# Leaving out the imaginary weight of mode 0 in a banded attention and spectral mixing kernel

## The chip, the cores and the metric

The kernel runs on one core of a Trainium2 chip. The metric is the device time of one execution in microseconds (us); of several executions the median is given. The engines are named as in the profile: PE (TensorE, matrix products; PEld its weight loads), DVE (VectorE), ACT (ScalarE), POOL (GpSimd) and SP (SyncE, which here only issues DMAs). POOL also issues DMAs, on a queue of its own, and these can change the type on the way from float32 to bfloat16.

## The reference

Attention over 8 batches, 8 heads, 576 tokens and 64 values per head, each token seeing itself and the 127 before it, gives x. Then comes mixing in the frequency domain of the token axis, and a last layer:

```python
X = np.fft.rfft(x, axis=1)
Xr, Xi = (np.real(X[:, :n_modes]), np.imag(X[:, :n_modes]))
Yr = np.einsum('bmd,mde->bme', Xr, w_r) - np.einsum('bmd,mde->bme', Xi, w_i)
Yi = np.einsum('bmd,mde->bme', Xr, w_i) + np.einsum('bmd,mde->bme', Xi, w_r)
Y[:, :n_modes] = Yr + 1j * Yi
y = np.fft.irfft(Y, n=S, axis=1)
u = x + y
return (u + np.maximum(u @ w_ch, 0.0)).astype(np.float32)
```

There are 64 modes, and each has a real and an imaginary weight, w_r and w_i, of 512 x 512 float32 values, that is 1 MB (1024 KB) each and 128 MB together. For mode 0 the sum over tokens has no imaginary part, so Xi is zero there, and the inverse real transform does not read the imaginary part of Y at mode 0. In mode 0 w_i therefore stands only in one product with zero and in one value that is not read.

## The kernel before

**Two stages.** The first computes attention for 16 units (a batch and half of the heads each) in a software pipeline and leaves x and its spectrum XC in the on-chip memory. The second, the weight stage, multiplies XC with the 128 weights in order, transforms back and writes the output in a closing stage (from L695 on).

**The order of the work.** Every engine runs its instructions in the order in which the program text issues them; the schedule is written by hand. The buffers of a pool are used in turn, and a load into a used buffer waits until the matmuls on its old content are done.

**Weights and their numbers.** Weight i is w_r of mode i/2 where i is even and w_i of mode (i-1)/2 where i is odd. The list todo_w (L438) holds the numbers that are not loaded yet. load_w(n, pool, bf16, chosen) (L440) takes the next n of the list that are not in the list again, or those in chosen. With bf16 it issues the load on POOL's queue into a bfloat16 tile (L449), 512 KB; without, on SP's queue into a float32 tile of 1024 KB (L453), of which the matmuls read the upper halves as bfloat16. wq keeps the tile of each number, homes the pool.

**What is loaded where.**
- During attention, at stages that AHEAD names (L413), 14 weights go by POOL's queue into the pool early, each (but the first) behind a small copy (gate, L520) that waits for a result of the pipeline. In the stages that LATER names, 6 more go into the tiles that held q, k and v. That is 20.
- After attention SP loads into the six buffers of the pool w (NWA = 6, L533). The first number that is left is called first, and again (L532) is the list of eight numbers first + 4, first + 6, ... that POOL will load into early a second time.
- In the weight loop, after the four matmuls of weight k: as long as k < AGAIN = 8, POOL reloads an early buffer (L656); for a weight in a buffer of SP's, SP loads the next into it (L658).
- K1 (L640) is the number behind the last of again. After weight K1 - 1 the memory of early is given up; two more buffers w2 for SP and the tile wch (by POOL) are put there.

**The weight loop** (L641). Four modes share one accumulator acc of 128 rows; mode m works on 32 of them, in the group of 32 columns of PE that belongs to them (tile_position). For each weight PE does four matmuls, with a part of XC as the loaded operand:

```python
m, ri = 4 * g + i // 2, i % 2
w = wq[2 * m + ri]
for a in range(4):
    nc.tensor.matmul(acc[32 * (i // 2) : 32 * (i // 2) + 32], lhsT=XC[...], rhs=w[a],
                     start=(ri == 0 and a == 0), stop=(ri == 1 and a == 3),
                     tile_position=(0, 32 * (i // 2)))
```

After eight weights quad_end scales acc to yq (DVE at L543, ACT at L541 for the last), PE transposes it (L547), and DVE copies it to YT. From weight 64 on a list of other work, side, is taken piece by piece between the weights: four early_spectra (L575) and 36 project (L613), which multiply tokens by w_ch. After each of weights 123 to 126, where the list is empty, PE gets six matmuls whose result is not used (warm, L633).

Of the kernel before, what the change touches and what calls it, by code (L numbers as in the profile page):

```python
# [397 lines left out]
def kernel(  # L398
# [13 lines left out]
    NM, DM, _ = moe_w_r.shape  # L412
    AHEAD = {0: 1, 1: 1, 2: 1, 4: 1, 5: 1, 7: 1, 8: 1, 10: 1, 11: 1, 12: 1, 13: 3, 14: 1}  # L413
    LATER = {14: 3, 15: 3}
    EARLY, NWA, NWB, AGAIN = 14, 6, 2, 8
# [12 lines left out]
    early = actx1.enter_context(  # L428
        tc.tile_pool(name="w1", bufs=EARLY, side="right", reuse_waits="tile")
    )  # L430
# [4 lines left out]
    vflat = raw["v"].rearrange("p u s h d -> p (u s h d)")  # L435
    spare += [vflat[:, 2 * DM * i :] for i in range(3)]
    spare = [t[:, : 2 * DM].bitcast(BF16).rearrange("p (a e) -> p a e", a=4) for t in spare]
    wq, homes, todo_w, again = {}, {}, list(range(2 * NM)), []  # L438

    def load_w(n, pool, bf16, chosen=None):  # L440


        for i in ([i for i in todo_w if i not in again][:n] if chosen is None else chosen):
            todo_w.remove(i)
            src = (moe_w_r, moe_w_i)[i % 2][i // 2].rearrange("(p a) e -> p a e", a=4)
            homes[i] = pool
            if bf16:
                t = spare.pop(0) if pool is None else pool.tile([P, 4, DM], BF16, tag="w", name="w")
                nc.gpsimd.dma_start(out=t, in_=src)  # L449
                wq[i] = [t[:, a] for a in range(4)]  # L450
            else:
                t = pool.tile([P, 4, DM], FP32, tag="w", name="w")
                nc.sync.dma_start(out=t, in_=src)  # L453
                wq[i] = [t[:, a].bitcast(BF16)[:, 1::2] for a in range(4)]

    with ExitStack() as actx:
# [43 lines left out]
        for h in (0, 2):  # L500
# [4 lines left out]
        side = {0: [(at.offset, 4), (at.offset, 6), (at.decay, 5), (at.offset, 5), (at.decay, 7),  # L505
                    (at.offset, 7), (at.decay, 4), (at.decay, 6)]}
# [18 lines left out]
    with ExitStack() as mctx:  # L525
# [6 lines left out]
        again = [first + 4 + 2 * i for i in range(AGAIN)]  # L532
# [4 lines left out]
        def quad_end(acc, g):  # L537

            yq = pool.tile([P, DM], BF16, tag="yq")
            if g == NM // 4 - 1:  # L540
                nc.scalar.mul(yq, acc, 2.0 / S)  # L541
            else:
                nc.vector.tensor_scalar_mul(yq, acc, 2.0 / S if g else norm)  # L543
            yield
            tr = ps.tile([P, 4, P], BF16, tag="tr", bufs=1, name="tr")
            for et in range(4):
                nc.tensor.transpose(tr[:, et], yq[:, et * P : (et + 1) * P], ident)  # L547
            hf, mm = g // 8, 4 * (g % 8)
            for ri in range(2):
                src = tr.rearrange("p e (j c) -> p e c j", c=32)[:, :, ri * B : ri * B + B]  # L550
                dst = YT[:, hf, :, :, ri, mm : mm + 4]
                if hf == 1:
                    nc.vector.tensor_copy(dst, src)
                else:
                    for par in range(2):
                        nc.vector.tensor_copy(dst[:, :, 1 - par :: 2], src[:, :, par::2])
# [76 lines left out]
        def warm():  # L633
            wt = ps.tile([P, DM], FP32, tag="warm", bufs=1, name="warm")
            for _ in range(6):
                nc.tensor.matmul(wt, lhsT=ident, rhs=wch[:, 0], start=True, stop=True)  # L636

        quads, side = [], []
        ZW = Z = XW = wch = w2 = None
        K1 = again[-1] + 1  # L640
        for g in range(NM // 4):  # L641
            acc = ps.tile([P, DM], FP32, tag="acc", bufs=2, name="acc")
            for i in range(8):
                m, ri = 4 * g + i // 2, i % 2
                w = wq[2 * m + ri]
                for a in range(4):
                    c0 = (a * NC + (8 if ri == 0 else 0)) * NM + m
                    nc.tensor.matmul(  # L648
                        acc[32 * (i // 2) : 32 * (i // 2) + 32],
                        lhsT=XC[:, c0 : c0 + 31 * NM + 1 : NM],  # L650
                        rhs=w[a],
                        start=(ri == 0 and a == 0), stop=(ri == 1 and a == 3),
                        tile_position=(0, 32 * (i // 2)),
                    )
                k = 8 * g + i
                if k < AGAIN:  # L656
                    load_w(1, early, True, again[k : k + 1])
                elif homes[k] not in (early, None):  # L658
                    load_w(1, homes[k], False)
                if k == K1 - 1:  # L660
                    actx1.close()
                    w2 = mctx.enter_context(
                        tc.tile_pool(name="w2", bufs=NWB, side="right", reuse_waits="tile")
                    )
                    load_w(NWB, w2, False)
                    right = mctx.enter_context(
                        tc.tile_pool(name="late", bufs=1, side="right", reuse_waits="tile")
                    )
                    wch = right.tile([P, 4, DM], BF16, name="wch")
                    nc.gpsimd.dma_start(out=wch, in_=moe_w_ch.rearrange("(a p) e -> p a e", p=P))  # L670
                    ZW = right.tile([P, B // 2, 2, DM], BF16, name="ZW")
                    Z = right.tile([P, B, DM], BF16, name="Z")
                    XW = right.tile([P, len(units), 2, DM], BF16, name="XW")

                if quads:
                    if next(quads[0], True):
                        quads.pop(0)
                elif side and k % 5:
                    side.pop(0)()
                elif 8 * g + i >= 2 * NM - 5:  # L680
                    if 8 * g + i < 2 * NM - 1:
                        warm()
            end = quad_end(acc, g)
            next(end)
            quads.append(end)
            if g == 7:
                side += [partial(early_spectra, bp) for bp in range(B // 2)]
                side += [partial(project, j, n) for j in range(len(units)) for n in range(2)]
# [132 lines left out]
```

The softmax here doesn't subtract the row's maximum and nothing guards it: scores larger than these inputs give would overflow.

## Time and profile before

| | |
|---|---|
| median of nine runs | 457.98 us (456.46 to 459.09) |
| the profiled execution's own time | 459.09 us |
| its span in the profile | 457.3 us |
| its mean granted PE clock | 0.906 of full speed |
| PE busy | 358.9 us (78%) |
| DVE, ACT, POOL busy | 173.6, 154.8, 54.3 us |
| matmuls of the weights, acc (L648) | 488 recorded as reading the tiles w, 145.7 us |
| DMA packets | 158.31 MB, mean 346 GB/s |
| SP's queue (hardware_dynamic) | 142.62 MB, 81.2% of 16 engines over the span |
| POOL's queue (software_dynamic) | 15.21 MB, 16.8% |
| issues of weights by SP | 54 of w_i and 46 of w_r, 1024 KB each, 18.7 and 18.3 us to landing (median) |
| issues of weights by POOL into early | 15 of w_r and 7 of w_i, 512 KB each; six more into the tiles of q, k and v |

Attention takes the first 134 us or so; the first matmul of a weight starts at 134.46 us and the last ones at 414.07 us.

How to read it: the span is the profiled stretch on the core; the execution's own time is a little longer. The lines of the profile give start and duration in us, the engine, the line of the kernel (L648 is line 648), the operation and the tiles that it writes and reads, then how often. A bracket behind a line holds the idle time of the engine before it and what ended that. The chain of waits is the sequence of work that ended last, followed back from the end.

### The profile page before, as it was taken

What the parts mean: (1) busy time and instruction counts of PE and PEld (TensorE: products, weight loads), DVE (VectorE), ACT (ScalarE), POOL (GpSimd) and SP (SyncE); (2) the same over time, 40 slices, a digit from 0 to 9 for tenths busy, and PEclk for the clock granted to TensorE, in tenths of its full rate; (3) what the DMA queues carried; (4) which work ended last, traced back from release to release, by engine and by line L of the source; (5) the groups of instructions that cost most, each with busy time, mean ns of one, the idle gap of its engine ahead of it and who ended that gap; (6) DMA issues with size and microseconds to landing.
All of it is one profiled execution on the core that took longest, in us unless ns stands there. A gap on an engine that the chain in (4) does not pass through costs nothing.

```text
span 457.3 us, 7803 instructions
## 1 busy us (share of the span) xinstructions
PE 358.9 (78%) x3269; PEld 189.5 (41%) x3292; DVE 173.6 (38%) x314; ACT 154.8 (34%) x191; POOL 54.3 (12%) x86
## 2 busy tenths in 40 slices
PE   5678999998867656566666799998989898987793
PEld 4456777776654212122221244443433343433230
DVE  7988699998832101000010142111111111202684
ACT  6869799998810000000000021121111121204572
POOL 8510001012402100000000000000000000000562
PEclk9989899999999778866677589999999899999998
DMA  8999999999999999999999999999999999990598
GB/s 281 323 335 302 293 257 314 314 301 240 203 286 315 313 318 316 335 387 425 420 421 419 423 421 418 420 421 421 421 419 420 421 421 418 421 412 24 191 346 290
DMA packets 51874, 158.31 MB, mean 346 GB/s; under 512 B 3712, under 2 KB 22656, under 8 KB 39040
## 3 DMA queue, kind: packets, MB, share of 16 engines
q1 hardware_dynamic: 47280, 142.62, 81.2%
q0 software_dynamic: 4560, 15.21, 16.8%
q8 instruction: 25, 0.41, 0.4%
q14 instruction: 9, 0.07, 0.0%
HBM read 163.58 MB, written 9.44 MB: 378 GB/s over the span
## 4 chain that ended last, share of the span: by engine, by line
DMA 56%; PE 24%; DVE 10%; ACT 4%; issue 3%; POOL 1%; ACTq 0%; DVEq 0%; POOLq 0%; SPq 0%
DMA w<-in_moe_w_i_dram 33%; DMA w<-in_moe_w_r_dram 13%; PE acc L648 7%; DMA vr<-in_moe_w_i_dram 6%; DMA qr<-in_q_dram 5%; PE av L332 3%; PE my L623 2%; PE tp L251 2%; DVE x L348 1%; DVE vb L234 1%; DVE q L239 1%; DVE o L766 1%; PE warm L636 1%; PE yy L752 1%; DVE att L306 1%
## 5 line engine op out<-in xcount | busy, mean ns | idle before, releaser
L648 PE MATMUL acc<-w,XC 128*32 128x512 bf16 x488 | 145.7, 449 | 53.6 <-DMA w<-in_moe_w_r_dram 34.6
L648 PEld LDWEIGHTS <-XC 128*32 128x32 bf16 x512 | 59.6, 140 | 128.0 <-issue 95.7
L295 ACT ACTIVATE att<-sc 128x1024 bf16<-128x1024 f32 x64 | 64.1, 1033 | 9.6 <-PE sc L285 9.6
L629 ACT CAST XW<-my 128x512 bf16<-128x512 f32 x36 | 21.1, 587 | 108.0 <-PE my L587 108.0
L733 POOL TENSOR_TENSOR r<-r,x 128x1024 f32<-128x1024 f32 x8 | 17.0, 2131 | 274.2 <-ACT r L731 274.1
L571 ACT CAST ZW<-zw 128x512 bf16<-128x512 f32 x4 | 2.3, 587 | 137.0 <-PE zw L566 137.0
L543 DVE TENSOR_SCALAR yq<-acc 128x512 bf16<-128x512 f32 x14 | 9.7, 690 | 98.6 <-PE acc L648 98.6
L611 DVE COPY xT<-tr 128x1024 bf16<-128x1024 bf16 x18 | 12.5, 692 | 89.5 <-PE tr L609 89.5
L332 PE MATMUL av<-vb,att 128*128 128x132 bf16 (+1 forms) x576 | 38.4, 217 | 8.1 <-DVE x L348 5.4
L332 PEld LDWEIGHTS <-att 128*128 128x128 bf16 x704 | 36.6, 98 | 13.5 <-DVE x L348 9.9
L623 PE MATMUL my<-wch,xT 128*64 128x512 bf16 x288 | 38.7, 391 | 0.8 <-DVE xT L611 0.8
L257 ACT COPY qkT<-tp 128x1152 bf16<-128x1152 bf16 x30 | 33.5, 1118 | 3.2 <-PE tp L251 2.5
L285 PE MATMUL sc<-qkT 64*64 64x256 bf16 (+2 forms) x640 | 25.3, 265 | 5.1 <-ACT qkT L257 1.2
L348 DVE TENSOR_TENSOR x<-av,rec 128x640 bf16<-128x640 f32 x32 | 26.4, 825 | 1.1
L766 DVE TENSOR_TENSOR o<-yy,r 128x1024 f32<-128x1024 f32 (+1 forms) x20 | 21.8, 1115 | 8.0 <-PE yy L752 3.9
L623 PEld LDWEIGHTS <-xT 128*64 128x64 bf16 x288 | 13.4, 110 | 23.3 <-issue 9.9
L285 PEld LDWEIGHTS <-qkT 64*64 64x64 bf16 x640 | 14.6, 109 | 19.3 <-issue 16.3
L234 DVE CAST vb<-vr 64x1024 bf16<-64x1024 f32 x32 | 22.2, 694 | 0.2
L306 DVE TENSOR_TENSOR att<-att,mask 128x1024 bf16<-128x1024 bf16 x32 | 20.6, 685 | 0.0
L731 ACT ACTIVATE r<-mm 128x1024 f32<-128x1024 f32 (+1 forms) x19 | 17.8, 979 | 6.6 <-PE mm L587 6.5
L272 PE MATMUL sc<-bias,ident 128*128 128x512 bf16 x48 | 16.7, 402 | 1.4 <-ACT att L295 1.4
L520 POOL COPY gate<-x 1x1 bf16<-1x1 bf16 x11 | 5.4, 490 | 88.6 <-DVE x L348 88.6
(105 smaller groups left out, 333.1 us busy)
## 6 DMA issues: line engine op xcount, KB each, us to landing
w<-in_moe_w_i_dram SPq DMA_DIRECT2D x54, 1024.0 KB, 18.7
w<-in_moe_w_r_dram SPq DMA_DIRECT2D x46, 1024.0 KB, 18.3
qr<-in_q_dram SPq DMA_DIRECT2D x16, 576.0 KB, 8.6
kr<-in_k_dram SPq DMA_DIRECT2D x16, 576.0 KB, 8.5
vr<-in_v_dram SPq DMA_DIRECT2D x32, 256.0 KB, 7.6
w<-in_moe_w_r_dram POOLq DMA_DIRECT2D x15, 512.0 KB, 21.2
out_dram<-o SPq DMA_DIRECT2D x15, 512.0 KB, 3.8
w<-in_moe_w_i_dram POOLq DMA_DIRECT2D x7, 512.0 KB, 8.3
```

Source lines behind the costliest of these rows:

```text
L234: nc.vector.tensor_copy(self.vb[u % 2][row, :, :, :, W * half : W * half + D], src[row, :2])
L257: (self.nc.vector.tensor_copy if u < 2 and w == "q" else self.nc.scalar.copy)(dst.rearrange("q h (p j) -> q h p j", j=TPP), tp.rearrange(" ...
L285: nc.tensor.matmul(sc[64 * half : 64 * half + 64, e, j * 256 + c0 : j * 256 + c0 + n], lhsT=qkT[row, 1, h, k0 + j : k0 + P : 2], rhs=qkT[r ...
L295: self.nc.scalar.activation(self.att[u % 2][:, kt * 8 * P : (kt + 1) * 8 * P], sc.rearrange("p e n -> p (e n)"), AF.Exp, scale=1.0 / math. ...
L306: nc.vector.tensor_tensor(out=rows, in0=rows, in1=self.table[:, heads], op=ALU.mult)
L332: nc.tensor.matmul(bank[:, qt * W : qt * W + rhs[j].shape[1]], lhsT=att[:, o : o + P], rhs=rhs[j], start=(n == 0 and j == 0), stop=(n == l ...
L348: nc.vector.tensor_tensor(out=self.x[:, b, :, cs].rearrange("p t (h d) -> p h t d", h=2), in0=tiles[:, :, :, :D], in1=rec.unsqueeze(-1).br ...
L623: nc.tensor.matmul(mm[ROWS[half]], lhsT=lhsT, rhs=wch[:, dt], start=(dt == 0), stop=False, skip_group_check=True,)
L629: nc.scalar.copy(XW[:, j, n], mm)
L648: nc.tensor.matmul(acc[32 * (i // 2) : 32 * (i // 2) + 32], lhsT=XC[:, c0 : c0 + 31 * NM + 1 : NM], rhs=w[a], start=(ri == 0 and a == 0), ...
L731: nc.scalar.activation(r[:, part], mm[:, part], AF.Relu)
L766: nc.vector.tensor_tensor(out=o[:, c], in0=yy[:, c], in1=r[:, c], op=ALU.add)
```

## The change

Number 1, which is w_i of mode 0, is taken out of todo_w. In the loop a number that was never loaded is passed over before its matmuls, with all that stands behind it in the loop's body. Since weight 0 is then the only one of mode 0, its fourth matmul ends the accumulation. The reloads no longer go by the number k < 8 but by a copy of again, recycle, of which each weight that is multiplied takes one until it is empty.

```diff
-    wq, homes, todo_w, again = {}, {}, list(range(2 * NM)), []
+    wq, homes, todo_w, again = {}, {}, [0, *range(2, 2 * NM)], []
@@
-        quads, side = [], []
+        quads, side, recycle = [], [], list(again)
@@
                 m, ri = 4 * g + i // 2, i % 2
+                if 2 * m + ri not in wq:
+                    continue
                 w = wq[2 * m + ri]
@@
-                        start=(ri == 0 and a == 0), stop=(ri == 1 and a == 3),
+                        start=(ri == 0 and a == 0), stop=(ri == (m > 0) and a == 3),
@@
                 k = 8 * g + i
-                if k < AGAIN:
-                    load_w(1, early, True, again[k : k + 1])
+                if recycle:
+                    load_w(1, early, True, [recycle.pop(0)])
                 elif homes[k] not in (early, None):
```

The lists that follow from todo_w, worked out from the text of both kernels:

| | before | after |
|---|---|---|
| loaded during attention (20) | 0 to 19 | 0, 2 to 20 |
| first | 20 | 21 |
| again (8, by POOL) | 24, 26, ... 38 | 25, 27, ... 39 |
| K1 | 39 | 40 |
| loaded by SP | 100 | 99 |

## The prediction

> **What bounds the kernel now.** I read the page from its slices down. The rows for TensorE (PE), the granted clock, the DMA engines and their rate, 40 slices of 11.43 us each:
>
> ```profile
> PE   5678999998867656566666799998989898987793
> PEclk9989899999999778866677589999999899999998
> DMA  8999999999999999999999999999999999990598
> GB/s 281 323 335 302 293 257 314 314 301 240 203 286 315 313 318 316 335 387 425 420 421 419 423 421 418 420 421 421 421 419 420 421 421 418 421 412 24 191 346 290
> ```
>
> The DMA row is full until slice 36. From slice 18 (206 us) the rate is flat at 418 to 425 GB/s, and it does not move when PE goes from six tenths busy to nine, nor when the clock goes from 0.5 to 0.9. A rate that ignores PE is set by the transfers. Before slice 17 it is lower, 313 to 318 GB/s, with the DMA row just as full: both queues run there. The windows of the weight stage say the same (span, busy time and count of PE, PEld, DVE, ACT and POOL, granted clock, DMA share, rate):
>
> ```profile
> 153.00:192.00 39.00, 23.49 (x83) 9.03 (x80) 2.62 (x10) 0.00 (x0) 0.82 (x2) 0.78 1.04 318
> 192.00:214.00 22.00, 13.51 (x41) 4.84 (x40) 1.31 (x5) 0.00 (x0) 0.00 (x0) 0.70 1.04 400
> 235.00:256.00 21.00, 14.50 (x40) 4.57 (x38) 1.31 (x5) 0.00 (x0) 0.00 (x0) 0.66 1.01 422
> 300.00:350.00 50.00, 44.35 (x287) 19.81 (x288) 7.20 (x13) 8.22 (x14) 0.00 (x0) 1.00 1.01 421
> ```
>
> Then the chain of waits, to see what PE does when a weight arrives. In 192 to 256 us it alternates a DMA of 18 us with four matmuls; its end is this:
>
> ```profile
> 385.33 18.75 DMA w<-in_moe_w_i_dram
> ...
> 404.13 1.07 PE acc L648 x4
> ...
> 405.35 1.24 PE warm L636 x5
> ...
> 406.61 1.07 PE acc L648 x4
> 407.68 1.40 PE warm L636 x6
> ...
> 409.10 1.07 PE acc L648 x4
> ...
> 414.07 1.08 PE acc L648 x4
> ```
>
> The last wait for a transfer ends at 404.13, with weight 123. From there PE runs weight, warm burst, weight without a gap, one per (414.07 - 404.13) / 4 = 2.485 us, which is also the pace of the transfers. Behind 415 us lies a closing stage of 42 us that reads no weight. So the end is: arrival of weight 123, plus a fixed tail.
>
> **The change, part by part.** I number weights 2m for w_r and 2m + 1 for w_i of mode m. Weight 1 drops out of the list todo_w. Since load_w takes the next of the list and not a named one, no issue place goes empty in the attention stage: the POOL issue at 25.42 us, until now weight 1, fetches weight 2, and so on down the list.
>
> Attention stage: 20 loads of 512 KB written, before and after, at the same places: 0. Only their numbers shift (now 0, 2 to 20).
>
> Reloads: "again" was 24, 26, ... 38 (w_r of modes 12 to 19) and becomes 25, 27, ... 39 (w_i of the same modes). Still eight on POOL's queue, again at the first eight weights that PE finishes; K1 goes from 39 to 40, so that the w2 buffers and wch still come after the 39th weight consumed. By order of consumption (20 from stock, 4 by SP, then 8 by POOL alternating with SP, then SP alone) both kernels have the same pattern up to the 39th weight. The pace there is POOL's queue sharing the engines with SP's: PE is released by a reload every 4.97 us:
>
> ```profile
> 181.91 1.93 PE L648 MATMUL acc<-w,XC 128*32 128x512 bf16 x8 [0.98 <-DMA w<-in_moe_w_r_dram]
> 186.89 3.25 PE L648 MATMUL acc<-w,XC 128*32 128x512 bf16 x8 [3.06 <-DMA w<-in_moe_w_r_dram]
> 191.86 1.93 PE L648 MATMUL acc<-w,XC 128*32 128x512 bf16 x8 [1.72 <-DMA w<-in_moe_w_r_dram]
> ```
>
> The last, at 191.86, is number 38 now and 39 then, and in either case the 39th consumed. So at 191.86 us both kernels stand at the same point: 89 weights remain before, 88 after.
>
> SP's queue: 100 loads become 99. The missing one falls out of the stretch after 191.86, where SP's queue alone fills the engines. Its price: 1024 KB = 1.0486 MB at 421 GB/s is 2.49 us; the pace of 2.485 us at the end agrees. Bounds: from below 2.47 us (the fastest slice, 425 GB/s); from above the mean of the whole queue, 81.2% of 457.3 us for 142.62 MB, or 2.73 us for this size, which includes the small pieces of q, k and v. I take 2.49, since the rows of the very stretch give it.
>
> PE: four matmuls and four weight loads of mode 0 fall away near 135 us. The 36 matmuls from 134.46 take 4.76 us, so four are 0.53 us. Cover: PE then waits for stock anyway, 3.94 us at 152.06 for weight 19. So 0; were the cover gone it would be a gain of 0.53 us. The second reload on POOL could be issued 0.5 us sooner, but POOL's later issues (142.59, 147.58, 152.54) wait for its own older DMAs, which set the pace: 0. SP has one issue less, 0.33 us against a spacing of 2.49: 0. No wait is added; the accumulation of mode 0 only ends at its fourth matmul.
>
> One thing is new: after a reload PE now takes w_i of one mode and then w_r of the next, in another group of 32 columns, where it took both of one mode in the same group. The eight above take 1.93 us; at 142.25 to 144.26 us sixteen matmuls of alternating groups took 2.0 us, so eight would take 1.0 and a buffer of SP's come free up to 0.93 us sooner. The engines are full (share 1.04), so I take 0; the bounds are 0 and a gain of 0.93 us, were the issue of 193.82 us to come into empty engines.
>
> Other order: the quad ends (L541, L543) come one consumed weight sooner. ACT and DVE are idle there (2.62 us of DVE in 39 us): 0. The side work starts at k = 64, still 64 weights from the end, and so moves with the stream.
>
> Sum: -2.49 us. The profiled execution took 459.09 us (span 457.3, 1.79 around it) and would take 456.60. It was the slowest of the nine runs, 1.11 us over their median; the median 457.98 becomes **455.49 us**, -0.54%.
>
> Here the Trainium skill differs: "DMA: Bandwidth & Descriptors", Specifications, gives a limit of some 358 GB/s from HBM for one core, by which the transfer would be worth 2.93 us and the estimate would be 455.05. The trace holds 421 GB/s for 200 us, so the measurement decides.
>
> **The rivals.** A. *Nothing comes of it.* What is left out was hidden: it was issued at 25.42 us, under attention's compute. If one of those 20 early loads were missing and SP still had 100, the time would stay at 457.98. Against: the instruction order has 99 weight issues on SP and as many as before on POOL. What remains of it is a late loss, PE's lag below of 1.7 us, which leaves -0.8 us, 457.2: within 0.2% (0.92 us, about what these nine runs can tell from no change).
>
> B. *Slower: PE's clock drops in the last five weights.* From 404.13 to 415 PE has no slack: 1.07 + 1.40 + 0.02 = 2.49 us a weight. Such drops exist:
>
> ```profile
> 256.00:264.00 8.00, 6.73 (x18) 1.98 (x18) 1.31 (x5) 0.00 (x0) 0.00 (x0) 0.50 1.01 421
> 360.00:368.00 8.00, 6.67 (x36) 2.43 (x35) 0.00 (x0) 0.88 (x2) 0.00 (x0) 0.79 1.02 420
> ```
>
> The second costs 8 x 0.21 = 1.7 us of PE and is caught up by 404, where PE again waits 1.43 us for a transfer. Moved to the end it takes most of the gain (case A). The first, 8 us at 0.50, costs 4.0 us there: 457.98 - 2.49 + 4.0 = 459.5. It decides slower from a lag of 2.49 + 0.92 = 3.4 us. For it: one weight fewer shifts all that follows by 2.49 us, and with it where drops fall. Against: in that stretch the granted clock is 1.00 and the warm bursts are there in both kernels.
>
> "TensorE: Matmul & The Clock Gate", HAM oscillation, in the skill says that idle gaps of PE over about 3.4 us throttle it. Here the clock sank to 0.66 in 235 to 256 us, where the timeline has idle gaps of 0.6 to 1.4 us before a weight, so the rule doesn't tell where a drop falls; by it there would be none at the end and the sum would stand.
>
> C. *More than forecast.* The pairing in two column groups gives its 0.93 us, and the transfer 2.73: 457.98 - 3.66 = 454.3.
>
> **How the numbers follow.** Forecast, 1.7 to 3.2 us gained: 0.80. A, within 0.2%: 0.10. B: 0.06. C: 0.04. Faster by over 0.2% is forecast and C, 0.84; same 0.10; slower 0.06. The range goes from C's end, 454.3, to 457.0, where the gain would just be told from nothing; it leaves out B and most of A. The forecast's own: 454.8 to 456.3.
>
> **What would show it.** Right: up to 190 us the changed trace lies on the old one, with POOL's last reload, now of w_i, landing near 191.9; flat 421 GB/s after it; SP with 99 weight issues; the last wait of acc for a transfer near 401.6 instead of 404.13, the last acc near 411.6 instead of 414.07, and from there to the end 42 to 43 us as before. Wrong: a reload landing a step of 4.97 us later, a rate under 418 GB/s after 206 us, or a PE that no longer waits for any transfer in the last twenty weights.

## The result, and the profile after

The changed kernel takes 454.04 us (median of 21 runs, 453.2 to 456.06) and the kernel before, run beside it, 457.41 us (63 runs). The ratio is 0.9934, with a 95% interval of 0.9922 to 0.9946: 3.0 us less, between 2.5 and 3.6; the two medians alone lie 3.4 us apart. Forecast were 2.49 us less and 455.5 us, in a range of 454.3 to 457.0. The median of 454.04 us lies 0.26 us under that range. The forecast starts from a median of nine runs, 457.98, and the kernel before took 0.57 us less in the 63 runs here; the ratio applied to 457.98 gives 454.96, inside the range.

The slices of the page after (PE busy, granted clock, DMA engines, rate; 40 slices of 11.3 us):

```profile
PE   4688999999866535367676789998988898987793
PEclk8689999999989665555656699999999999999998
DMA  8999999999999999999999999999999999990598
GB/s 283 320 326 314 312 293 311 319 292 243 211 302 312 301 318 317 345 395 426 418 422 421 421 422 420 418 425 417 422 421 420 417 422 419 423 391 12 204 348 285
```

The picture is the same: a full DMA row, 301 to 318 GB/s while both queues load, then some 420 GB/s to the end of the weights. What differs is PE in slices 13 to 16 (147 to 192 us, the first slice being 0): it is less busy and has a lower clock. The windows say it in numbers (columns as before):

```profile
153.00:192.00 39.00, 17.66 (x89) 7.97 (x86) 3.31 (x11) 0.00 (x0) 0.75 (x1) 0.59 1.04 320
192.00:214.00 22.00, 15.64 (x41) 4.76 (x40) 1.77 (x9) 0.00 (x0) 0.00 (x0) 0.52 1.03 410
235.00:256.00 21.00, 14.06 (x38) 4.37 (x36) 1.31 (x5) 0.00 (x0) 0.00 (x0) 0.66 1.01 420
300.00:350.00 50.00, 43.54 (x283) 19.71 (x283) 7.20 (x13) 7.97 (x14) 0.00 (x0) 1.00 1.01 421
```

From 153 to 192 us PE was busy 23.49 us at a clock of 0.78 before; now it is 17.66 us at 0.59. The rate did not fall (318 to 320 GB/s).

The queues and the issues of weights, from the page after:

```profile
q1 hardware_dynamic: 47136, 141.57, 81.2%
...
w<-in_moe_w_r_dram SPq DMA_DIRECT2D x53, 1024.0 KB, 18.4
w<-in_moe_w_i_dram SPq DMA_DIRECT2D x46, 1024.0 KB, 18.5
```

SP's queue moves 141.57 MB instead of 142.62: 1.05 MB, one weight less, 99 issues. The timeline of PE at the last reloads and the end of the chain of waits, both of the kernel after:

```profile
179.15 1.94 PE L650 MATMUL acc<-w,XC 128*32 128x512 bf16 x8 [3.07 <-DMA w<-in_moe_w_i_dram]
184.09 1.94 PE L650 MATMUL acc<-w,XC 128*32 128x512 bf16 x8 [3.00 <-DMA w<-in_moe_w_i_dram]
189.10 1.94 PE L650 MATMUL acc<-w,XC 128*32 128x512 bf16 x8 [3.08 <-DMA w<-in_moe_w_i_dram]
```

```profile
380.55 18.45 DMA w<-in_moe_w_i_dram
399.04 1.07 PE acc L650 x4
400.27 1.24 PE warm L636 x5
401.53 1.07 PE acc L650 x4
402.59 1.40 PE warm L636 x6
...
408.98 1.08 PE acc L650 x4
```

The last wait for a transfer ends at 399.04 instead of 404.13. From there to the end of the span it is 53.2 us in both traces. But the two traces differ by 5.09 us at that point, and the change did not bring all of it: the first matmul of acc is at 131.51 us instead of 134.46, so 2.95 us come from attention, in which the same work is done. From the first matmul of acc to the last wait for a transfer it is 269.67 us before and 267.53 after: 2.14 us in this pair of traces. A single trace of each kernel is too few for a difference of 2.5 us, and the experiments were read by this stretch as well as by their ratios. Here are the points of all traces, each read from the timeline of PE; the kernels e1 to e12 are those of the experiments below:

| kernel | SP's loads | first acc | last reload | last wait | first acc to last wait | ratio to before |
|---|---|---|---|---|---|---|
| before | 100 | 134.46 | 191.86 | 404.13 | 269.67 | |
| e1_load_kept | 100 | 132.26 | 191.68 | 402.66 | 270.40 | 0.9990 (0.9968 to 1.0012) |
| e3_early_slot_empty | 100 | 132.65 | 191.29 | 402.66 | 270.01 | 0.9995 (0.9974 to 1.0017) |
| after | 99 | 131.51 | 189.10 | 399.04 | 267.53 | 0.9934 (0.9922 to 0.9946) |
| e9_changed_again | 99 | 130.96 | 189.30 | 398.81 | 267.85 | 0.9941 (0.9922 to 0.9961) |
| e2_multiply_kept | 99 | 131.28 | 188.67 | 398.30 | 267.02 | 0.9927 (0.9901 to 0.9953) |
| e5_real_reloads | 99 | 133.18 | 190.74 | 400.38 | 267.20 | 0.9945 (0.9925 to 0.9966) |
| e6_warm_four | 99 | 133.20 | 190.65 | 400.60 | 267.40 | 0.9959 (0.9940 to 0.9977) |
| e11_warm_eight | 99 | 132.59 | 191.88 | 400.08 | 267.49 | 0.9996 (0.9970 to 1.0022) |
| e4_eight_more | 91 | 132.30 | 189.78 | 379.54 | 247.24 | 0.9498 (0.9469 to 0.9526) |
| e10_one_load_twice | 99 | 133.24 | 191.32 | 400.81 | 267.57 | 0.9963 (0.9945 to 0.9981) |
| e12_load_twice_again | 99 | 135.46 | 191.53 | 401.78 | 266.32 | 0.9962 (0.9941 to 0.9983) |
| e8_one_k_buffer | 99 | 135.60 | | 403.82 | 268.22 | 1.0013 (0.9993 to 1.0032) |
| e7_fifteen_early | 98 | 137.14 | | 402.54 | 265.40 | 0.9963 (0.9948 to 0.9979) |

The last wait is that of weight 123 in all of them. In e7 and e8 PE's waits near 190 us are for weights of SP's and not for reloads, so that point is left out.

### The profile page after: what moved, and what is told of

Same layout as the page of the kernel before. It is cut to its first block, busy times and chain, and to the rows that moved or that the text cites. A ratio compares the mean times of both kernels' runs of the same rounds, so it can differ in the third digit from the quotient of the medians.

```text
span 452.2 us, 7793 instructions
## 1 busy us (share of the span) xinstructions
PE 349.9 (77%) x3265; PEld 185.3 (41%) x3288; DVE 173.4 (38%) x314; ACT 154.5 (34%) x191; POOL 54.7 (12%) x86
## 3 DMA queue, kind: packets, MB, share of 16 engines
q1 hardware_dynamic: 47136, 141.57, 81.2%
## 4 chain that ended last, share of the span: by engine, by line
DMA 56%; PE 23%; DVE 12%; ACT 4%; issue 3%; SPq 0%; ACTq 0%; POOL 0%; DVEq 0%; POOLq 0%
DMA w<-in_moe_w_i_dram 42%; PE acc L650 7%; DMA vr<-in_moe_w_i_dram 6%; DMA w<-in_moe_w_r_dram 6%; PE av L332 3%; PE my L623 2%; DVE x L348 2%; DVE vb L234 2%; DMA qr<-in_q_dram 2%; DVE att L306 2%; DVE k L239 1%; DVE o L768 1%; PE warm L636 1%; DVE q L239 1%; PE tp L251 1%
## 5 line engine op out<-in xcount | busy, mean ns | idle before, releaser
L650 PE MATMUL acc<-w,XC 128*32 128x512 bf16 x484 | 137.2, 469 | 55.1 <-DMA w<-in_moe_w_i_dram 37.3
L650 PEld LDWEIGHTS <-XC 128*32 128x32 bf16 x508 | 57.2, 141 | 126.8 <-issue 102.8
L332 PEld LDWEIGHTS <-att 128*128 128x128 bf16 x704 | 36.5, 98 | 11.3 <-DVE x L348 8.3
L234 DVE CAST vb<-vr 64x1024 bf16<-64x1024 f32 x32 | 22.2, 694 | 0.2
```

The source lines that it names most:

```text
L234: nc.vector.tensor_copy(self.vb[u % 2][row, :, :, :, W * half : W * half + D], src[row, :2])
L332: nc.tensor.matmul(bank[:, qt * W : qt * W + rhs[j].shape[1]], lhsT=att[:, o : o + P], rhs=rhs[j], start=(n == 0 and j == 0), stop=(n == l ...
```

## The experiments

### The load or the matmuls

Two kernels split the change. In the first, weight 1 is loaded in its old place and only its multiplication is left out:

```diff
-    wq, homes, todo_w, again = {}, {}, [0, *range(2, 2 * NM)], []
+    wq, homes, todo_w, again = {}, {}, list(range(2 * NM)), []
-                if 2 * m + ri not in wq:
+                if 2 * m + ri == 1:
                     continue
```

> Weight 1 is loaded as before (20 loads in attention, 100 by SP, reloads 24 to 38), but its four matmuls are left out. Theory of the stream (the end is set by the bytes of SP's queue, one transfer is 2.49 us): the four matmuls (0.53 us) are hidden by the wait for stock, so no change to the kernel before, ratio 0.999 to 1.001. Rival, that the matmuls are what paid (or the 0.5 us by which the measured gain of 3.0 us lies over 2.49): ratio 0.9988 or lower, down to 0.993.

Measured: 457.5 us, ratio 0.9990 (0.9968 to 1.0012). In the second it is not loaded, but PE does four matmuls in its place:

```diff
-                if 2 * m + ri not in wq:
-                    continue
-                w = wq[2 * m + ri]
+                k = 8 * g + i
+                w = wq[2 if k == 1 else k]
 ...
-                        start=(ri == 0 and a == 0), stop=(ri == (m > 0) and a == 3),
+                        start=(ri == 0 and a == 0), stop=(ri == 1 and a == 3),
 ...
-                k = 8 * g + i
-                if recycle:
+                if k == 1:
+                    pass
+                elif recycle:
```

> Weight 1 is not loaded (99 by SP, as in the changed kernel), but PE still does its four matmuls, on the tile of weight 2, so that the output differs in the part of mode 0 that is not read or is multiplied by zero. Theory of the stream: the whole gain stays, ratio 0.993 to 0.9946 to the kernel before. Rival, that the matmuls paid: ratio 0.998 to 1.0.

Measured: 454.42 us, ratio 0.9927 (0.9901 to 0.9953). Without the matmuls but with the load the time is that of the kernel before, and with the matmuls but without the load the gain is whole: the load pays, and the matmuls pay nothing that shows (the interval of the first run would leave them at most 1.5 us). The changed kernel itself, run again, gives the size once more:

> The changed kernel as it is, for comparison on the same chip and for a second trace. Ratio to before 0.992 to 0.995; in the trace, first matmul of acc to the last wait of acc for a transfer 267 to 268 us, against 269.7 to 270.4 in the three traces with 100 loads by SP.

Measured: 454.8 us, ratio 0.9941 (0.9922 to 0.9961), and 267.85 us in the trace.

### Which transfer is saved

The next kernel leaves the place of weight 1 empty instead of moving the list up.

```diff
-    AHEAD = {0: 1, 1: 1, 2: 1, 4: 1, ...}
+    AHEAD = {0: 1, 2: 1, 4: 1, ...}
```

> Weight 1 is not loaded, but the list does not move up: attention loads one weight less (19, nothing at the stage where weight 1 was fetched), and SP still loads 100. Theory of the stream with attention as cover (case A of the prediction): the early load was hidden, SP's 100 transfers stay, ratio 0.999 to 1.001. Rival, that the engines are the bound through attention as well, so that any transfer left out anywhere pays its engine time: 2.5 us, ratio 0.993 to 0.995.

Measured: 457.49 us, ratio 0.9995 (0.9974 to 1.0017). Its page has SP's queue as before:

```profile
q1 hardware_dynamic: 47280, 142.62, 81.6%
```

So the same weight not loaded is worth nothing that shows (at most 1.2 us by the interval) where its early load is what falls out, and the full price where the list moves up and SP's last part gets shorter. The time comes from the move.

### The price of one transfer

The next kernel leaves out nine weights instead of one, so that the price of each can be read more exactly.

```diff
+    DROP = {1, *range(41, 57, 2)}
-    ... todo_w, again = {}, {}, [0, *range(2, 2 * NM)], []
+    ... todo_w, again = {}, {}, [i for i in range(2 * NM) if i not in DROP], []
-                if 2 * m + ri not in wq:
+                if 2 * m + ri in DROP:
                     continue
 ...
-                        start=(ri == 0 and a == 0), stop=(ri == (m > 0) and a == 3),
+                        start=(ri == 0 and a == 0), stop=(ri == (2 * m + 1 not in DROP) and a == 3),
```

> The changed kernel with eight more weights neither loaded nor multiplied (w_i of modes 20 to 27, numbers 41 to 55, all from the stretch where SP alone loads), so that the output lacks their part. Theory of the stream: each is worth one transfer, 8 x 2.49 = 19.9 us below the changed kernel, 434.1 us for 454.0, ratio to before 0.949 to 0.951. If each is worth the 3.0 us that the change gave: 430.0 us, ratio 0.940. If PE or its clock becomes the bound in that stretch (1.9 us a weight at the low clock): less than 16 us, ratio over 0.958.

Measured: 434.98 us, ratio 0.9498 (0.9469 to 0.9526). By the medians that is 22.2 us less than the kernel before on the same chip (457.14 us) for nine weights, 2.46 us each; by the ratio it is 22.9 us, 2.55 us each (2.41 to 2.70). SP's queue on its page:

```profile
q1 hardware_dynamic: 45984, 133.18, 80.3%
```

That is 8.39 MB less than after, eight weights. By the traces, the mean stretch from the first acc to the last wait is 267.42 us (267.02 to 267.85) in the six with 99 loads by SP and attention as in the changed kernel (after, e2, e5, e6, e9, e11), so eight transfers take (267.42 - 247.24) / 8 = 2.52 us each; and the mean of the three with 100 loads is 270.03, 2.61 us above. The 3.0 us per weight that the ratio of the change would suggest are ruled out, and so is the other price in the prediction, 2.93 us: nine weights would then end at 430 and 430.8 us.

### Two weights in one column group or in two

The change swaps the reloads from real to imaginary weights. This kernel swaps them back. The reloads thereby stand one place earlier: three of SP's weights come ahead of them instead of four, and K1 is 39 instead of 40; the last of them is the 38th weight consumed and not the 39th.

```diff
-        again = [first + 4 + 2 * i for i in range(AGAIN)]
+        again = [first + 3 + 2 * i for i in range(AGAIN)]
```

> The changed kernel, but the eight reloads are again the real weights (24, 26, ... 38 instead of 25, 27, ... 39), so that after a reload PE takes both weights of one mode in one group of 32 columns, as in the kernel before; still 127 weights, 99 by SP. Theory of the stream alone: as the changed kernel, ratio 0.993 to 0.995. Rival, that the pairing of two column groups gave the part of the gain over 2.49 us: less gain, ratio 0.9945 to 0.996, and in the trace some 0.3 to 0.5 us more from the first matmul of acc to the last wait of acc for a transfer (267.2 us in the three traces with reloaded imaginary weights, 270.0 less 2.5 = 267.5 expected here).

Measured: 455.4 us, ratio 0.9945 (0.9925 to 0.9966), and 267.20 us in the trace, no more than the others with 99 loads. The ratio lies in both expectations and does not tell them apart; the trace speaks for the first, though it is a single one and the others with 99 loads differ by up to 0.8 us. So the pairing is worth nothing that shows. The window from 165 to 190 us, here of before, of after and of this run, shows what it does to PE:

```profile
165.00:190.00 25.00, 14.40 (x44) 5.38 (x44) 1.31 (x5) 0.00 (x0) 0.00 (x0) 0.77 1.04 317
```

```profile
165.00:190.00 25.00, 10.37 (x48) 4.54 (x46) 1.31 (x5) 0.00 (x0) 0.00 (x0) 0.50 1.04 324
```

```profile
165.00:190.00 25.00, 14.45 (x44) 5.33 (x44) 1.31 (x5) 0.00 (x0) 0.00 (x0) 0.79 1.04 319
```

With real reloads PE is busy 14.4 us of 25 at a clock of 0.77 to 0.79; with imaginary ones, where it interleaves two groups, it is busy 10.4 us and the clock is 0.50. Two bursts of the kernel after show how it comes to this:

```profile
159.25 1.16 PE L650 MATMUL acc<-w,XC 128*32 128x512 bf16 x8 [1.45 <-DMA w<-in_moe_w_i_dram]
164.18 1.93 PE L650 MATMUL acc<-w,XC 128*32 128x512 bf16 x8 [3.78 <-DMA w<-in_moe_w_i_dram]
```

At 159.25 us the eight matmuls take 1.16 us at a clock of 1.00, near the 1.0 estimated. In the gap of 3.78 us behind them the clock falls to 0.50, and there it stays, so that the eight at each arrival up to 189 us take 1.93 us. In the kernel before, in one group, eight take 1.93 us where the clock is 1.00 (181.91 and 191.86 us) and 3.25 us where it is low, mean 0.57 (186.89 us), in turn. So the lower clock takes back a part of what the interleaving gave. At about every other arrival PE is still done 1.3 us sooner, and SP's buffers with it, and yet the stretch to the last wait is no shorter: the transfers (share 1.04 in all three windows) set the pace.

### The last five weights

In the last 10 us PE seems to have no slack. The next two kernels ask whether PE or the transfers set the end there.

```diff
-            for _ in range(6):
+            for _ in range(4):
                 nc.tensor.matmul(wt, lhsT=ident, rhs=wch[:, 0], start=True, stop=True)
```

> The changed kernel with four instead of six warm matmuls behind each of weights 123 to 126 (their result is not used). If PE sets the last 10 us (1.07 + 1.40 us a weight, no gap) and the last transfer is there up to 1 us before its matmuls, as the rate of the DMA engines suggests (it falls to 8 GB/s by 408 us, last matmuls at 408.98): 0.5 to 1.0 us less than the changed kernel, ratio to before 0.991 to 0.9925. If the transfers set it: same as the changed kernel, 0.993 to 0.9945. If the idle gaps lower the granted clock in the closing stage: slower, 0.996 or more.

Measured: 455.26 us, ratio 0.9959 (0.9940 to 0.9977): no gain. The ratio lies between the second and the third expectation. From the last wait to the end of the span it is 52.9 us, no more than the 53.2 of before and after, so the trace shows no slower closing stage. The timeline of PE in this run shows why nothing was gained:

```profile
403.09 1.07 PE L650 MATMUL acc<-w,XC 128*32 128x512 bf16 x4 [0.45 <-DMA w<-in_moe_w_r_dram]
404.09 1.04 PE L636 MATMUL warm<-wch,ident 128*128 128x512 bf16 x4
405.57 1.07 PE L650 MATMUL acc<-w,XC 128*32 128x512 bf16 x4 [0.44 <-DMA w<-in_moe_w_i_dram]
406.57 1.04 PE L636 MATMUL warm<-wch,ident 128*128 128x512 bf16 x4
408.05 1.07 PE L650 MATMUL acc<-w,XC 128*32 128x512 bf16 x4 [0.44 <-DMA w<-in_moe_w_r_dram]
...
410.52 1.07 PE L650 MATMUL acc<-w,XC 128*32 128x512 bf16 x4 [0.44 <-DMA w<-in_moe_w_i_dram]
```

Each of the last weights still comes every 2.48 us, and PE now waits 0.44 us for it. I had taken from the falling rate that the last weight lies ready. It does not: in this run the mean share of the 16 DMA engines is 0.63, 0.44 and 0.17 in the three microseconds from 407 to 410, and PE still waits for a transfer until 410.52. That some engines are done while others still move the last weight would explain it; no view here shows the engines one by one. The counter-test has eight warm matmuls (the same line, range(8)):

> The changed kernel with eight instead of six warm matmuls behind each of weights 123 to 126. The run with four showed a wait of 0.44 us for a transfer before each of the last four weights, which is just two warm matmuls (0.43 us): with six PE is level with the transfers. With eight PE sets the end (case B's place): 4 x 0.43 = 1.7 us later than the changed kernel, ratio 0.9965 to 0.9985, and in the trace 2.9 us between the last weights instead of 2.49. If there were slack left: as the changed kernel, 0.9925 to 0.9955.

Measured: 457.1 us, ratio 0.9996 (0.9970 to 1.0022). Its timeline of PE:

```profile
402.91 1.12 PE L650 MATMUL acc<-w,XC 128*32 128x512 bf16 x4
403.96 1.90 PE L636 MATMUL warm<-wch,ident 128*128 128x512 bf16 x8
405.79 1.12 PE L650 MATMUL acc<-w,XC 128*32 128x512 bf16 x4
406.84 1.90 PE L636 MATMUL warm<-wch,ident 128*128 128x512 bf16 x8
```

There is no wait any more, and a weight comes every 2.88 us; from weight 123 to the last one it takes 11.47 us (400.08 to 411.55) instead of 9.94. So the trace shows 1.5 us of loss in these weights, and 0.4 us more behind them (43.65 us from the last weight to the end of the span, 43.22 in after). The ratio lies somewhat above what was expected (2.8 us over the changed kernel), though its interval holds it. With six, PE is level with the transfers to some 0.02 us a weight: two warm matmuls fewer give a wait of 0.44 us, and they take 0.43.

### One more early load

If attention covers early loads, a further one should save another transfer of SP. The memory had no room for it without other cuts:

```diff
-    EARLY, NWA, NWB, AGAIN = 14, 6, 2, 8
+    EARLY, NWA, NWB, AGAIN = 15, 5, 3, 8
-    AHEAD = {0: 1, 1: 1, 2: 1, 4: 1, ...}
+    AHEAD = {0: 1, 1: 1, 2: 1, 3: 1, 4: 1, ...}
-            dst = self.mid.tile([P, TPP, 2, D], BF16, tag=w, name=w)
+            dst = self.mid.tile([P, TPP, 2, D], BF16, tag=w, bufs=1 + (w == "q"), name=w)
 ... (the order of the steps)
-    ("cast", "k", -2), ("exp", 2, 0), ("norm", 0, 1), ("cast", "q", -3), ("score", 3, 0),
+    ("exp", 2, 0), ("norm", 0, 1), ("cast", "k", -2), ("cast", "q", -3), ("score", 3, 0),
```

> The changed kernel with one more weight loaded during attention (21 instead of 20, at the stage after 33 us, into a fifteenth early buffer), so that SP loads 98. To make room, the pool w has five buffers instead of six and w2 three instead of two, and the cast k has one buffer instead of two (its cast stands two steps later in the stage). Theory of the stream with attention as cover: one more transfer leaves the stretch after the reloads, 2.5 us less than the changed kernel, 451.5 us, ratio to before 0.988. If attention has no room for 512 KB more, or pays for the one buffer of k: ratio 0.993 or more.

Measured: 455.29 us, ratio 0.9963 (0.9948 to 0.9979), no better than the changed kernel. The stretch from the first matmul of acc to the last wait is shorter, 265.40 us, but attention is longer. The control has the cuts without the extra load:

> The run with fifteen early loads without its extra load: the changed kernel with 14 early buffers, but the pool w with five buffers, w2 with three, and the cast k with one buffer. It tells which part of that run made attention end near 137.1 us instead of 131 to 133.2 (first matmul of acc). If the single buffer of k (and the later cast) did: first matmul of acc near 136 us or later, ratio to before 0.998 to 1.002. If the extra 512 KB did: first matmul at 131 to 133.2, ratio 0.992 to 0.996.

Measured: 457.46 us, ratio 1.0013 (0.9993 to 1.0032). The first matmul of acc in each, the run with fifteen buffers first:

```profile
137.14 3.88 PE L650 MATMUL acc<-w,XC 128*32 128x512 bf16 x32 [1.34 <-ACT XC L392]
```

```profile
135.60 3.89 PE L650 MATMUL acc<-w,XC 128*32 128x512 bf16 x32 [1.34 <-ACT XC L392]
```

The cuts cost 0.7 to 0.8% (1.0013 against 0.9934 and 0.9941) and so eat the gain: against its control the extra load is worth 0.9963 / 1.0013 = 0.995, about 2.3 us. In the two traces the stretch behind attention is 2.8 us shorter with it (265.40 against 268.22 us), but its first matmul of acc is 1.5 us later. To see what the extra load itself costs attention, the changed kernel got one more load that brings nothing, weight 0 a second time:

```diff
+    twice = []
 ...
+                if i == 0:
+                    twice.append((t, src))
 ...
+            if stage == 3:
+                ...
+                nc.gpsimd.dma_start(out=twice[0][0], in_=twice[0][1])
             if stage in AHEAD:
```

> The changed kernel with one more load of 512 KB in attention and nothing else: at the stage after 33 us POOL fetches weight 0 a second time into the same tile, behind a gate of its own. If attention covers such a load (as the run with one load less suggests): as the changed kernel, ratio 0.992 to 0.9955, first matmul of acc at 131 to 133.5 us. If the engines have no room for it: 2.5 us later, ratio 0.998 to 1.0, first matmul at 134 us or later.

Measured: 455.49 us, ratio 0.9963 (0.9945 to 0.9981), between the two expectations. So it was run once more:

> The run with weight 0 loaded twice once more, since 0.9963 (0.9945 to 0.9981) lay between the two expectations. If attention covers 512 KB more: 0.992 to 0.9955; if it pays 2.5 us: 0.998 to 1.0; again between them (0.9955 to 0.998): it covers a part of it.

Measured: 455.91 us, ratio 0.9962 (0.9941 to 0.9983), first matmul of acc at 135.46 us (133.24 in the first; two traces of one kernel can lie that far apart). Against 0.9934 and 0.9941 the ratio of both is 1.0 to 1.3 us more, though the intervals overlap. That reads as partial cover, which is not shown: a load less in attention gained nothing that shows, and a load more cost less than its price of 2.5 us, but is perhaps not free. No version was found that beats the changed kernel.

## Why the prediction was right

Right in direction, mechanism and price, with these points:

- **SP's transfer as the price (2.49 us).** Shown: 2.46 us a weight by the medians of the run with nine weights less, 2.55 by its ratio, 2.52 by the traces of eight, 2.61 between 100 and 99 loads. The change itself measured 3.0 us, and its interval from 2.5 to 3.6 begins where the price lies; the repeat gave 2.7 (1.8 to 3.6). Whether anything stands behind the other 0.5 us is open. In the traces the first matmul of acc comes 1.0 us sooner on average in the six with 99 loads than in the three with 100 (132.12 against 133.12 us), but each group scatters by 2.2 us, so this may be chance.
- **455.49 us.** Missed by 1.45 us: 0.57 of it is the starting point, a median of only nine runs that lay high, and the rest is the gain, 3.4 us by the medians instead of 2.49. That the median fell below case C's 454.3 does not make case C right: of its two grounds the pairing gave nothing that shows, and a price of 2.73 us a transfer lies just above the interval of 2.41 to 2.70.
- **Attention 0.** Shown by the empty early slot, for a load that is left out there. Its condition, that the list moves up, decides between the full gain and none: case A was right about the load and wrong about the kernel.
- **PE's matmuls 0.** Shown from both sides, within the intervals given above.
- **The pairing 0, at most 0.93 us.** No gain showed, and the reason given, full engines, fits the traces. The price of the pairing was read too simply: the prediction took 1.93 us for eight matmuls in one group, but one of the three lines that it shows has 3.25, and it left out that the clock would change with the pairing.
- **Up to 190 us one trace lies on the other.** Wrong as stated. The first matmul of acc came 2.95 us sooner and the last reload at 189.10. The first ten traces of the table, of which only e3 has another attention stage, scatter from 130.96 to 134.46 us at the first matmul of acc. The stretch from there to the last reload is alike in these two traces, 57.59 us after and 57.40 before, but runs from 57.39 to 59.42 over the same ten.
- **Rate after 206 us.** A rate under 418 GB/s was named as a sign of being wrong. Two slices of the page after read 417 (slice 35, in which the stream runs out, left aside), but the mean from 300 to 350 us is 421 in both kernels; the sign was drawn too close.
- **End of the chain.** The last wait was foreseen near 401.6 and came at 399.04; with the 2.95 us of attention added back it would be 401.99. The fixed tail held.
- **Case B.** It did not come: the clock was 1.00 in the last weights. Its ground was right, PE has no slack there; two matmuls a weight more cost 1.5 us in the trace.

The rule on idle gaps in the Trainium skill ("TensorE: Matmul & The Clock Gate", HAM oscillation), over about 3.4 us, fits the clock here only in part. The kernel after fell from 1.00 to 0.50 in a gap of 3.78 us, near 161.7 us, but the kernel before fell near 163.4 us behind a gap of 2.52; and the kernel after then stayed at 0.50 up to 189 us with gaps of 3.1 us at most.

## What to carry to other kernels

In a stream that fills the DMA engines, count the transfers behind the last point at which both kernels stand alike; here a load left out paid only where the list behind it moved up into the freed place. Work saved on an engine that waits for the stream anyway, here PE's four matmuls, paid nothing that shows. For differences of half a per cent compare a stretch between two fixed events in several traces, not two spans.

## What the runs showed of the hardware

Interleaving matmuls of two groups of 32 columns lowered PE's busy time in the 25 us from 165 to 190 us: it was between 14.4 and 15.5 us in one group (before, e1, e3, e5) and some 10.4 in two (after, e2, e4, e6, e9, e10, e11; 12.2 in e12), while an arrival came every 5 us. The granted clock, between 0.65 and 0.79 in the first group, was 0.50 in the second. Eight matmuls in two groups take 1.93 us at nearly every arrival (2.3 in e12); in one group, in the kernel before, they take 1.93 us at a clock of 1.00 and 3.25 to 3.46 us at the low one. In the kernel before the bursts at the low clock last that long and the clock is back at 1.00 within 0.6 us of their end (near 170.2 and 190.7 us); in the kernel after they last 1.94 us and it does not come back before 189 us. That the longer burst is what brings the clock back fits these traces, but no run tested it.

At the end of the stream, in the run with four warm matmuls, the mean rate over 16 engines is 426 GB/s from 406 to 407 us and 262, 180 and 57 GB/s in the three microseconds to 410, while the last weight is used only from 410.52 us, behind a wait for a transfer: a falling rate was no sign that the last weight was there.
